# A scheduled attention-and-MLP kernel: the second products four tiles behind, new prices in the planner, variance's small steps on GpSimd

## The chip, the cores and the metric

The kernel runs on one core of a Trainium2 chip. The metric is device time in microseconds (us). The engines are TensorE (PE in the profile; PEld is its weight loading), VectorE (DVE), ScalarE (ACT), GpSimd (POOL) and the engine that issues most loads, SyncE (SP).

## What is computed

Two stages follow one another. The first is attention over 4 batches, 8 heads, 768 positions and 64 numbers a head: each query sees the keys less than 16 positions away, and 24 summary keys, one for each block of 32 positions (the maximum of the block's keys; its value is the mean of the block's values). The second takes the heads side by side as 3072 rows of 512 numbers.

```python
k_sum = k.reshape(B, H, nb, block, D).max(axis=3)
v_sum = v.reshape(B, H, nb, block, D).mean(axis=3)
scores_l = where(|i - j| < 16, scale * q @ k.T, -1e9)
scores_s = scale * q @ k_sum.T + log(block)
a = softmax(concat(scores_l, scores_s))
x = a @ concat(v, v_sum)               # 3072 x 512 after the heads are joined
h = x @ w_in                           # 512 -> 1024
solu = h * softmax(h)
ln = (solu - mean) / sqrt(var + 1e-6) * g_ln
out = ln @ w_out                       # 1024 -> 512
```

## The kernel before

**Tiles.** The 3072 rows are 24 tiles of 128 rows, six to a batch. Attention works in steps: a batch has three groups `g` of 256 queries, a group two steps `pp`, each for two pairs of heads. So there are 24 attention steps too. For a step, `scores` copies the windows of the keys from `kraw` and the block maxima from `ksum` into one buffer `kw` (lines 530 to 538), multiplies (`s`, line 551), adds the mask and takes the maximum (line 571), takes exponentials (line 579) and divides by the sum (line 586, recorded at lines 263 and 264). `values_turn` transposes the result on TensorE (`t`) and copies it (`at`); `values` multiplies by the values (`x`, line 646) and splits the product into a high and a low part (`xh`, `xl`, line 652).

**A tile of the second stage** has three parts. `first(t)` makes `h` as 24 matmuls into two PSUM banks, since each product is done three times, high by low, low by high and high by high (line 671). Then follow row maximum (681), exponential (686), the multiply by `h` and 1/sum (694), the subtraction of the mean in two halves (702 on GpSimd, or 704 on VectorE), the sum of squares (707), and the small steps on one number a row that give 1/std `y`: scale and add (709), power -0.5 on GpSimd (712), and one correction step on VectorE (714, 716, 718). `turn(t)` transposes the centred tile `he` (`lt`) and splits it into `lh` and `ll` (732). `second(t)` makes the 24 matmuls of the output (`o`, line 747), scales them by `y` (`os`, 752 or 754) and stores them. Only `os` needs `y`.

**Distance.** In the loop over `t`, `turn` is called for tile `t - LAG + 1` and `second` for `t - LAG`; `LAG` is 5. The centred tile stays in one of `NHE` = 6 buffers `he` until `turn` has read it. Up to `t` = 5 (`NEAR`) the order around `first` is another than after it. The `h` banks and the banks shared by `x` and `o` are given out by `place_h` and `place_x`.

**Weights** come as 64-bit numbers in 16 pieces. Each is put together, rounded and split by `rounded` (lines 343 to 362) and then by `split_w_in` or `split_w_out` (375, 377); the eight output pieces are prepared during tiles 0 to 3. For `w_in` the staging buffers are the `he` buffers.

**The order of the work is made by a planner, `Plan`.** Every operation is recorded with an engine, a cost in us, the buffers that it reads and writes, and sometimes other engines that could do it (`alt`). `issue` then goes through a simulated time: for each engine it takes the operation that can begin first, and among those the one that is due first by what TensorE needs. An operation with a choice goes where its begin plus its cost plus a surcharge (`DEAR`: VectorE 0.3, ScalarE 0.3, GpSimd nothing) is least. Operations marked `port` are taken not to run on VectorE and GpSimd at one time. The result is a fixed order for each engine. Where the planner sees TensorE free before 80 us, `keep_up` puts in matmuls on zeros (line 863).

**Loads** go through SP's queue in program order. A batch's keys are loaded as four pairs `p`, at the tiles that `load_at` gives, and their block maxima are taken (`key_blocks`, line 414) at the tiles in `blocks_at`. For batches 2 and 3, GpSimd adds up the rows of the values (`add_rows`, lines 476 and 480).

Of the kernel before, what the change touches and what calls it, by code (L numbers as in the profile page):

```python
# [37 lines left out]
LAG = 5  # L38
NHE = 6
EARLY = 3  # L40
MEANS = 2
NEAR = 6
# [29 lines left out]
class Plan:  # L72
# [6 lines left out]
    RATE = 400.0  # L79
# [4 lines left out]
    DEAR = {"dve": 0.3, "act": 0.3}  # L84
# [53 lines left out]
    def issue(self):  # L138
# [50 lines left out]
        while len(order) < len(self.ops):  # L189
            t, e, o = min(((x[0], e, x[1]) for e in ready for x in [take(e)] if x),  # L190
                          key=lambda x: (x[0], x[2].due))
            for f in o.can:
                ready[f] = [x for x in ready[f] if x[1] is not o]
            then.pop(e, None)
            if o.then:
                then[e] = o.then
            o.start, o.engine, (o.cost, o.fn) = t, e, o.can[e]
            o.end = free[e] = t + cost(e, o, t)
            if e == "dve" and o.port:
                held = o.end  # L200
            if o.nbytes:
                dma = max(dma, o.end + 1.0) + o.nbytes / self.RATE * 1e-3
                o.end = dma + 0.8
            order.append(o)
            for u in o.users:
                u.left -= 1
                if not u.left:
                    enter(u)
# [21 lines left out]
def attn_then_solu(ctx: ExitStack, tc: tile.TileContext, q, k, v, vr, vb, w_in, w_out, g_ln, out):  # L230
# [98 lines left out]
    def load_w(key, src, after=()):  # L329
        raw[key] = x = plan.buf(const, [P, 1024], I32, f"w{key}", 1, f"raw{key}")  # L330
        op(sp, 0.05, lambda: nc.sync.dma_start(out=x.ap, in_=src.bitcast(I32)), w=[x], nbytes=P * 4096,
# [68 lines left out]
    def load_keys(b, p, after=()):  # L400
# [4 lines left out]
        op(sp, 0.05, lambda: nc.sync.dma_start(out=x.ap[:, i], in_=k[b, pp, :, i]), w=[(x, i)], nbytes=P * SP * 4,  # L405
# [12 lines left out]
    def load_v_rows(b, i):  # L418
# [3 lines left out]
        op(sp, 0.05, lambda: nc.sync.dma_start(out=x.ap, in_=vr[b, i]), w=[x], nbytes=P * 4096)  # L422
# [17 lines left out]
    def mean_values_pe(b):  # L440
# [18 lines left out]
        for g in range(4):  # L459
            op(act, 0.06, lambda g=g: nc.scalar.dma_start(  # L460
# [3 lines left out]
    def add_rows(b, hh, i):  # L464
# [3 lines left out]
        op(sp, 0.05, lambda w=w: nc.sync.dma_start(out=x.ap[:n, :w], in_=vb[b, hh, :, i * w:(i + 1) * w]),  # L468
# [30 lines left out]
    def load_q(b, g, pairs=None, after=()):  # L499
# [4 lines left out]
        op(sp, 0.05, lambda: nc.sync.dma_start(out=x.ap[:, part], in_=q[b, g, :, part]),  # L504
# [3 lines left out]
    def load_v(b, g, after=()):  # L508
        vt[b, g] = x = plan.buf(sb, [P, G, DM], F32, "vt", 2, f"vt{b}_{g}")
        op(sp, 0.05, lambda: nc.sync.dma_start(out=x.ap, in_=v[b, g]), w=[x], nbytes=P * 8192,  # L510
           after=after)

    def load_v2(b, g):
        x, y = vt[b, g], vsum[b]

        return op(act, 0.06, lambda: nc.scalar.dma_start(
# [3 lines left out]
    def scores(b, g, pp, each=False):  # L520

        nm_ = f"{b}_{g}_{pp}"
        kw = plan.buf(sb, [P, 2, G, KC], F32, "kw", 2, "kw" + nm_)
        x, y, qs = kraw[b, pp], ksum[b, pp], qt[b, g]

# [6 lines left out]
        for i in range(2) if each else [None]:  # L532
            i0, i1 = (0, 2) if i is None else (i, i + 1)
            f = (i1 - i0) / 2
            copy([(e, c * f + (1 - f) * 0.15) for e, c in COPY_K], lambda i0=i0, i1=i1: kw.ap[:, i0:i1, :, :WIN],
                 lambda i0=i0, i1=i1: window(i0, i1), r=[x if i is None else (x, i)], w=[(kw, (i, 0))], port=True)
            copy([(e, c * f + (1 - f) * 0.15) for e, c in COPY_KS], lambda i0=i0, i1=i1: kw.ap[:, i0:i1, :, WIN:],
                 lambda i0=i0, i1=i1: maxima(i0, i1), r=[y if i is None else (y, i)], w=[(kw, (i, 1))], port=True)
# [7 lines left out]
        def mm(i):  # L546
            for up in range(G // 2):
                for cu in range(2):
                    for j in range(2):
                        u, n = 2 * up + cu, 2 * i + up  # L550
                        nc.tensor.matmul(  # L551
                            sc.ap[cu * QT:(cu + 1) * QT, j, n * KC:(n + 1) * KC],
                            qs.ap[j * D:(j + 1) * D, 2 * pp + i, u * QT:(u + 1) * QT],
                            kw.ap[j * D:(j + 1) * D, i, u, :], start=True, stop=True)
        if each:
            for i in range(2):
                op(pe, 0.66, lambda i=i: mm(i), r=[(qs, 2 * pp + i), (kw, (i, 0)), (kw, (i, 1))], w=[(sc, i)])
        else:
            yield 1.18, lambda: (mm(0), mm(1)), [(qs, 2 * pp), (qs, 2 * pp + 1), kw], [sc]
# [100 lines left out]
    def first(t):  # L660
# [15 lines left out]
        nm, nmu, ss, y2 = (sm(x) for x in ("hm", "nmu", "ss", "y2"))  # L676
# [23 lines left out]
        for hf in range(2):  # L700
# [4 lines left out]
                out=e.ap[:, sl], in0=e.ap[:, sl], scalar1=nmu.ap, scalar2=None, op0=ALU.add))])  # L705
# [3 lines left out]
        op(dve, 0.07, lambda: nc.vector.tensor_scalar(  # L709
            out=ss.ap, in0=ss.ap, scalar1=1.0 / DF, scalar2=1e-6, op0=ALU.mult, op1=ALU.add), w=[ss])  # L710

        op(pool, 0.46, lambda: nc.gpsimd.tensor_tensor(out=y.ap, in0=ss.ap, in1=mhalf, op=ALU.pow),
           r=[ss], w=[y])
        op(dve, 0.13, lambda: nc.vector.scalar_tensor_tensor(
            out=y2.ap, in0=y.ap, scalar=y.ap, in1=ss.ap, op0=ALU.mult, op1=ALU.mult), r=[y, ss], w=[y2])
        op(dve, 0.07, lambda: nc.vector.tensor_scalar(
            out=y2.ap, in0=y2.ap, scalar1=-0.5, scalar2=1.5, op0=ALU.mult, op1=ALU.add), w=[y2])
        op(dve, 0.07, lambda: nc.vector.tensor_tensor(out=y.ap, in0=y.ap, in1=y2.ap, op=ALU.mult),
           r=[y2], w=[y])
# [17 lines left out]
    def second(t):  # L737
# [3 lines left out]
        for cols in [slice(0, 256), slice(256, 512)] if t == NT - 1 else [slice(0, DM)]:  # L741
# [14 lines left out]
            op(act, 0.06, lambda os=os, cols=cols: nc.scalar.dma_start(  # L756
# [38 lines left out]
    load_at, blocks_at = ((0, 1, 2, 3), (-1, 0, 1, 1)), ((0, 1, 2, 3), (0, 1, 1, 2))  # L795

    def pairs(at, t):
        return [(b + 1, p) for b in range(B - 1) for p in range(NPAIR) if t == 2 * NG * b + at[b > 0][p]]

    step = lambda i: (*its[i // 2], i % 2)  # L800
    for t in range(NT):
# [3 lines left out]
        if not near:  # L805
            run(scores(*step(t + 2)))
# [100 lines left out]
```

## Time and profile before

| | us |
|---|---|
| runs of the kernel before | 416.07, 417.98, 419.96 (median 417.98) |
| the profiled execution | 415.89 |
| its span | 414.2 |
| first `h` matmul (line 671) begins | 34.74 |
| first `o` matmul (line 747) begins | 96.91 |

The page's span runs from the first to the last instruction. A row of a group has line, engine, operation, output <- input, shape and count; then the busy time in us and the mean duration in ns; then the idle time of the engine just before, and what ended it. A row of the timeline has begin and length in us. A row of a stretch has its begin and end, its length, the busy time of PE, PEld, DVE, ACT and POOL with the number of instructions, the granted TensorE clock, the share of the DMA engines and GB/s. A row of waits says who waited for whom: us in total, times, longest. [...]

### The profile page before, as it was taken

The numbers are of one execution on the slowest core, as the hardware profiler recorded it, in microseconds if no ns is written. First come the engines' busy times: TensorE is split into PE (matmuls) and PEld (weight loads), VectorE is DVE, ScalarE is ACT, GpSimd is POOL, SyncE is SP. The second block draws the span as 40 slices with busy tenths as digits, with TensorE's granted clock in tenths as the row PEclk, the third lists the DMA queues.
The fourth block names the chain that finished last, engine by engine and source line by source line (L and its number), as shares of the span: only waits on it lengthen the run. The fifth ranks groups of instructions, "written<-read, shape, count | busy, mean of one in ns | idle before, by whom it ended". The sixth has DMA issues, their size and how long they took to land.

```text
span 414.2 us, 9561 instructions
## 1 busy us (share of the span) xinstructions
PE 395.3 (95%) x3654; PEld 299.6 (72%) x3654; DVE 311.7 (75%) x1009; ACT 223.2 (54%) x699; POOL 95.6 (23%) x151
## 2 busy tenths in 40 slices
PE   7899998989996999998999999999999999999996
PEld 3347656557775788877878887788888888777776
DVE  3989988999999878678877768758867785667230
ACT  3967774958495574746547455564554622123110
POOL 4223204210579640125111011011101010111000
PEclk9999999999999899999999999999999999999999
DMA  7999991122393140264240410430400000000011
GB/s 270 413 413 349 339 360 45 53 103 71 112 349 113 41 180 2 75 205 116 83 145 18 138 53 27 154 65 26 121 29 27 25 2 27 25 27 25 27 51 52
DMA packets 14993, 49.23 MB, mean 119 GB/s; under 512 B 1836, under 2 KB 2092, under 8 KB 13412
## 3 DMA queue, kind: packets, MB, share of 16 engines
q1 hardware_dynamic: 10112, 40.12, 26.8%
q10 hardware_dynamic: 4836, 8.51, 6.9%
q8 instruction: 29, 0.48, 0.5%
q14 instruction: 16, 0.13, 0.1%
HBM read 40.11 MB, written 6.29 MB: 112 GB/s over the span
## 4 chain that ended last, share of the span: by engine, by line
PE 62%; DVE 4%; POOL 1%; DMA 1%; ACT 0%; issue 0%; DVEq 0%
PE o L747 29%; PE h L671 22%; PE x L646 3%; PE s L551 3%; PE lt L607 3%; PE t L607 2%; POOL st_v L476 1%; DMA st_v<-in_vb 1%; DVE ksum L414 1%; DVE he L694 0%; DVE ll L732 0%; DVE e L571 0%; DVE at L257 0%; DVE lh L257 0%; DVE hm L681 0%; DVE os L754 0%
## 5 line engine op out<-in xcount | busy, mean ns | idle before, releaser
L671 PE MATMUL h<-w,xh 128*128 128x512 f32 x384 | 128.8, 404 | 5.5 <-DVE he L694 5.3
L747 PE MATMUL o<-w,lh 128*128 128x512 f32 (+1 forms) x400 | 128.4, 392 | 0.3 <-DVE xl L652 0.3
L579 ACT ACTIVATE e<-e,nm 128x120 f32<-128x120 f32 x192 | 73.1, 385 | 36.3 <-DVE nm L571 36.1
L671 PEld LDWEIGHTS h<-w,xh 128*128 128x128 f32 x384 | 72.8, 189 | 26.9 <-DVE he L694 8.5
L747 PEld LDWEIGHTS o<-w,lh 128*128 128x128 f32 x400 | 74.0, 188 | 19.0 <-issue 2.1
L747 PE MATMUL o<-w,ll 128*128 128x512 f32 (+1 forms) x200 | 77.1, 386 | 0.0
L671 PE MATMUL h<-w,xl 128*128 128x512 f32 x192 | 76.1, 397 | 0.9 <-DVE xl L652 0.8
L702 POOL TENSOR_SCALAR he<-he,nmu 128x512 f32<-128x512 f32 x27 | 24.7, 918 | 112.7 <-DVE nmu L697 112.7
L681 DVE TENSOR_REDUCE hm<-h 128x1 f32<-128x512 f32 x48 | 32.8, 686 | 18.7 <-PE h L671 18.5
L671 PEld LDWEIGHTS h<-w,xl 128*128 128x128 f32 x192 | 36.5, 190 | 9.5 <-DVE xl L652 1.5
L747 PEld LDWEIGHTS o<-w,ll 128*128 128x128 f32 x200 | 37.6, 188 | 7.2
L686 ACT ACTIVATE he<-h,hm 128x512 f32<-128x512 f32 x48 | 32.7, 688 | 18.3 <-DVE hm L683 16.6
L256 ACT COPY at<-t 120x512 f32<-120x512 f32 x28 | 16.0, 586 | 48.9 <-PE t L607 34.5
L571 DVE CUSTOM_DVE_ANT_0 e<-s,mask 128x120 f32<-128x120 f32 x192 | 40.5, 275 | 0.0
L707 ACT ACTIVATE sq<-he 128x1024 bf16<-128x1024 f32 x24 | 25.2, 1051 | 24.3 <-POOL he L702 16.7
L579 ACT ACTIVATION_READ_ACCUMULATOR e<-e,nm 128x1 f32 x192 | 36.6, 191 | 0.0
L694 DVE SCALAR_TENSOR_TENSOR he<-h,hz,he 128x512 f32<-128x512 f32 x48 | 34.2, 744 | 0.2
L732 DVE TENSOR_TENSOR ll<-lt,lh 128x512 fp32r<-128x512 f32 x48 | 31.6, 678 | 1.2 <-ACT lh L256 1.2
L646 PE MATMUL x<-at,vt 120*64 120x64 f32 (+1 forms) x768 | 28.7, 226 | 1.8 <-ACT at L256 1.1
L257 DVE CAST lh<-lt 128x512 fp32r<-128x512 f32 x21 | 14.4, 688 | 20.9 <-ACT lh L256 20.8
L551 PE MATMUL s<-kw,qt 64*64 64x120 f32 x768 | 26.1, 272 | 3.9 <-POOL kw L258 1.8
L646 PEld LDWEIGHTS x<-at,vt 120*64 120x64 f32 (+1 forms) x768 | 24.7, 137 | 6.8 <-issue 2.2
(89 smaller groups left out, 507.9 us busy)
## 6 DMA issues: line engine op xcount, KB each, us to landing
vt<-in_v SPq DMA_DIRECT2D x12, 1024.0 KB, 6.9
kraw<-in_k SPq DMA_DIRECT2D x16, 400.0 KB, 9.3
out<-os ACTq DMA_DIRECT2D x23, 256.0 KB, 2.0
qt<-in_q SPq DMA_DIRECT2D x11, 512.0 KB, 5.1
raw<-in_w_in SPq DMA_DIRECT2D x8, 512.0 KB, 9.6
raw<-in_w_out SPq DMA_DIRECT2D x8, 512.0 KB, 9.4
st_v<-in_vr SPq DMA_DIRECT2D x6, 512.0 KB
st_v<-in_vb SPq DMA_DIRECT2D x8, 384.0 KB
```

Source lines behind the costliest of these rows:

```text
L551: nc.tensor.matmul(sc.ap[cu * QT:(cu + 1) * QT, j, n * KC:(n + 1) * KC], qs.ap[j * D:(j + 1) * D, 2 * pp + i, u * QT:(u + 1) * QT], kw.ap[ ...
L571: nc.vector.tensor_tensor_reduce(out=e.ap[:, n, :], in0=sc.ap[:, j, (2 * i + up) * KC:(2 * i + up + 1) * KC], in1=mask[:, mi, :], scale=-S ...
L579: nc.scalar.activation(out=e.ap[:, n, :], in_=e.ap[:, n, :], func=AF.Exp, bias=nm.ap[:, n:n + 1], scale=-1.0, accum_out=z.ap[:, n:n + 1])
L646: nc.tensor.matmul(xp()[j * D:(j + 1) * D, i, qs], vs.ap[:k, u, cs], at.ap[:k, u % 2, n[j] + u // 2, :], start=not apart, stop=not apart o ...
L671: nc.tensor.matmul(hp.ap, a.ap[:, c, ts], w.ap[:, i], start=(c == 0 and n == 0), stop=(c == NKC - 1 and n == 2))
L681: op(dve, 0.6, lambda i=i, hp=hp: nc.vector.tensor_reduce(out=nms.ap[:, i:i + 1], in_=hp.ap, op=ALU.max, axis=AX.X, negate=True), r=[hp], ...
L686: op(act, 0.71, lambda i=i, hp=hp: nc.scalar.activation(out=part(i), in_=hp.ap, func=AF.Exp, bias=nm.ap, accum_out=zs.ap[:, i:i + 1]), r=[ ...
L694: op(dve, 0.67, lambda i=i, hp=hp: nc.vector.scalar_tensor_tensor(out=part(i), in0=hp.ap, scalar=zs.ap[:, 0:1], in1=part(i), op0=ALU.mult, ...
L702: op(pool, 0.62, lambda sl=sl: nc.gpsimd.tensor_scalar(out=e.ap[:, sl], in0=e.ap[:, sl], scalar1=nmu.ap, scalar2=1.0, op0=ALU.add, op1=ALU ...
L707: op(act, 1.13, lambda: nc.scalar.activation(out=sq.ap, in_=e.ap, func=AF.Square, accum_out=ss.ap), r=[e], w=[sq, ss])
L732: op(dve, 0.6, lambda part=part, r=r: nc.vector.tensor_tensor(out=part(lo), in0=tp.ap[:, r], in1=part(hi).bitcast(F32), op=ALU.subtract), ...
L747: nc.tensor.matmul(o.ap[:, cols], a.ap[:, f, :], w.ap[:, i, cols], start=(f == 0 and n == 0), stop=(f == NFC - 1 and n == 2))
```

## The change

- `LAG` is 4 and `NHE` 5: `turn` and `second` are called one tile earlier, and there is one `he` buffer fewer.
- In the planner an issue of a load on SP costs 0.43 instead of 0.05, and issues on ScalarE's queue 0.34 or 0.8 instead of 0.06. Transfers run at 410 GB/s, or 270 in the first 6.9 us, instead of 400, and land 0.6 after their end instead of 0.8.
- The surcharges are VectorE 0.6, ScalarE 0.3, GpSimd 1.0.
- The subtraction of the mean may run on ScalarE too, and is marked `port`.
- Of the small steps of the variance, those that were on VectorE are on GpSimd: scale and add, three multiplies, one more scale and add, around the power that was there before. That makes five GpSimd instructions more and four VectorE instructions fewer for a tile.
- The first group's scores (batch 0, group 0) are made directly from `kraw` and `ksum`, with two matmuls in place of each one and without `kw`. `DIRECT` = 0 leaves all others as they were.
- `load_at` and `blocks_at` are worked out. For batch 1 the four loads stand at tiles 1, 2, 3, 3 instead of 0, 1, 2, 3 and the block maxima at 2, 3, 3, 4 instead of 0, 1, 2, 3; for batches 2 and 3 they come out as before.

The diff, without the further lines on which only 0.05 becomes 0.43:

```diff
@@ -35,10 +35,11 @@
...
-LAG = 5
-NHE = 6
+LAG = 4
+NHE = 5
...
+DIRECT = 0
@@ -76,12 +77,12 @@
...
-    RATE = 400.0
+    RATE, SLOW = 410.0, 270.0
...
-    DEAR = {"dve": 0.3, "act": 0.3}
+    DEAR = {"dve": 0.6, "act": 0.3, "pool": 1.0}
@@ -199,8 +200,9 @@
...
-                dma = max(dma, o.end + 1.0) + o.nbytes / self.RATE * 1e-3
-                o.end = dma + 0.8
+                dma = max(dma, o.end + 1.0)
+                dma += o.nbytes / (self.RATE if dma > self.COLD else self.SLOW) * 1e-3
+                o.end = dma + 0.6
@@ -328,7 +330,7 @@
...
-        op(sp, 0.05, lambda: nc.sync.dma_start(out=x.ap, in_=src.bitcast(I32)), w=[x], nbytes=P * 4096,
+        op(sp, 0.43, lambda: nc.sync.dma_start(out=x.ap, in_=src.bitcast(I32)), w=[x], nbytes=P * 4096,
@@ -457,7 +459,7 @@
...
-            op(act, 0.06, lambda g=g: nc.scalar.dma_start(
+            op(act, 0.34, lambda g=g: nc.scalar.dma_start(
@@ -501,27 +503,28 @@
...
-        op(sp, 0.05, lambda: nc.sync.dma_start(out=x.ap[:, part], in_=q[b, g, :, part]),
+        op(sp, 0.43, lambda: nc.sync.dma_start(out=x.ap[:, part], in_=q[b, g, :, part]),
...
-        op(sp, 0.05, lambda: nc.sync.dma_start(out=x.ap, in_=v[b, g]), w=[x], nbytes=P * 8192,
+        op(sp, 0.43, lambda: nc.sync.dma_start(out=x.ap, in_=v[b, g]), w=[x], nbytes=P * 8192,
...
-        return op(act, 0.06, lambda: nc.scalar.dma_start(
+        return op(act, 0.8, lambda: nc.scalar.dma_start(
...
-    def scores(b, g, pp, each=False):
+    def scores(b, g, pp, direct=False, each=False):
+
...
-        kw = plan.buf(sb, [P, 2, G, KC], F32, "kw", 2, "kw" + nm_)
...
+        kw = None if direct else plan.buf(sb, [P, 2, G, KC], F32, "kw", 2, "kw" + nm_)
@@ -529,13 +532,9 @@
...
-        for i in range(2) if each else [None]:
-            i0, i1 = (0, 2) if i is None else (i, i + 1)
-            f = (i1 - i0) / 2
-            copy([(e, c * f + (1 - f) * 0.15) for e, c in COPY_K], lambda i0=i0, i1=i1: kw.ap[:, i0:i1, :, :WIN],
-                 lambda i0=i0, i1=i1: window(i0, i1), r=[x if i is None else (x, i)], w=[(kw, (i, 0))], port=True)
-            copy([(e, c * f + (1 - f) * 0.15) for e, c in COPY_KS], lambda i0=i0, i1=i1: kw.ap[:, i0:i1, :, WIN:],
-                 lambda i0=i0, i1=i1: maxima(i0, i1), r=[y if i is None else (y, i)], w=[(kw, (i, 1))], port=True)
+        if kw:
+            copy(COPY_K, lambda: kw.ap[:, :, :, :WIN], lambda: window(0, 2), r=[x], w=[(kw, 0)], port=True)
+            copy(COPY_KS, lambda: kw.ap[:, :, :, WIN:], lambda: maxima(0, 2), r=[y], w=[(kw, 1)], port=True)
@@ -548,15 +547,19 @@
...
-                        nc.tensor.matmul(
-                            sc.ap[cu * QT:(cu + 1) * QT, j, n * KC:(n + 1) * KC],
-                            qs.ap[j * D:(j + 1) * D, 2 * pp + i, u * QT:(u + 1) * QT],
-                            kw.ap[j * D:(j + 1) * D, i, u, :], start=True, stop=True)
+                        ds = slice(j * D, (j + 1) * D)
+                        at = (g * G + u) * QT
+                        keys = [(0, x.ap[ds, i, at:at + WIN]), (WIN, y.ap[ds, i, :])] if direct else [(0, kw.ap[ds, i, u, :])]
+                        for c, ks in keys:
+                            c += n * KC
+                            nc.tensor.matmul(
+                                sc.ap[cu * QT:(cu + 1) * QT, j, c:c + ks.shape[-1]],
+                                qs.ap[ds, 2 * pp + i, u * QT:(u + 1) * QT], ks, start=True, stop=True)
...
-                op(pe, 0.66, lambda i=i: mm(i), r=[(qs, 2 * pp + i), (kw, (i, 0)), (kw, (i, 1))], w=[(sc, i)])
+                op(pe, 1.1, lambda i=i: mm(i), r=[(qs, 2 * pp + i), (x, i), (y, i)], w=[(sc, i)])
...
-            yield 1.18, lambda: (mm(0), mm(1)), [(qs, 2 * pp), (qs, 2 * pp + 1), kw], [sc]
+            yield 2.0 if direct else 1.18, lambda: (mm(0), mm(1)), [(qs, 2 * pp), (qs, 2 * pp + 1)] + ([x, y] if direct else [kw]), [sc]
@@ -673,7 +676,7 @@
...
-        nm, nmu, ss, y2 = (sm(x) for x in ("hm", "nmu", "ss", "y2"))
+        nm, nmu, ss = (sm(x) for x in ("hm", "nmu", "ss"))
@@ -702,21 +705,23 @@
...
-                out=e.ap[:, sl], in0=e.ap[:, sl], scalar1=nmu.ap, scalar2=None, op0=ALU.add))])
+                out=e.ap[:, sl], in0=e.ap[:, sl], scalar1=nmu.ap, scalar2=None, op0=ALU.add)),
+                (act, 0.57, lambda sl=sl: nc.scalar.activation(
+                    out=e.ap[:, sl], in_=e.ap[:, sl], func=AF.Identity, bias=nmu.ap))], port=True)
...
-        op(dve, 0.07, lambda: nc.vector.tensor_scalar(
+
+        mul = lambda to, x: op(pool, 0.3, lambda: nc.gpsimd.tensor_tensor(out=to.ap, in0=to.ap, in1=x.ap, op=ALU.mult), r=[x], w=[to])
+        op(pool, 0.3, lambda: nc.gpsimd.tensor_scalar(
...
-
...
-        op(dve, 0.13, lambda: nc.vector.scalar_tensor_tensor(
-            out=y2.ap, in0=y.ap, scalar=y.ap, in1=ss.ap, op0=ALU.mult, op1=ALU.mult), r=[y, ss], w=[y2])
-        op(dve, 0.07, lambda: nc.vector.tensor_scalar(
-            out=y2.ap, in0=y2.ap, scalar1=-0.5, scalar2=1.5, op0=ALU.mult, op1=ALU.add), w=[y2])
-        op(dve, 0.07, lambda: nc.vector.tensor_tensor(out=y.ap, in0=y.ap, in1=y2.ap, op=ALU.mult),
-           r=[y2], w=[y])
+        mul(ss, y)
+        mul(ss, y)
+        op(pool, 0.3, lambda: nc.gpsimd.tensor_scalar(
+            out=ss.ap, in0=ss.ap, scalar1=-0.5, scalar2=1.5, op0=ALU.mult, op1=ALU.add), w=[ss])
+        mul(y, ss)
@@ -753,7 +758,7 @@
...
-            op(act, 0.06, lambda os=os, cols=cols: nc.scalar.dma_start(
+            op(act, 0.34, lambda os=os, cols=cols: nc.scalar.dma_start(
@@ -770,11 +775,11 @@
...
-    op(sp, 0.05, lambda: nc.sync.dma_start(out=g_sb, in_=g_ln), w=[g_b], nbytes=P * 64)
+    op(sp, 0.43, lambda: nc.sync.dma_start(out=g_sb, in_=g_ln), w=[g_b], nbytes=P * 64)
...
-        run(scores(0, 0, pp, True))
+        run(scores(0, 0, pp, True, True))
@@ -792,10 +797,19 @@
...
-    load_at, blocks_at = ((0, 1, 2, 3), (-1, 0, 1, 1)), ((0, 1, 2, 3), (0, 1, 1, 2))
+    scored = lambda i: i - 2 if i - 2 < NEAR else max(NEAR - 1, i - 4)
+
+    load_at, blocks_at = {}, {}
+    for later in range(1, B):
+        for p in range(NPAIR):
+            t = scored(2 * NG * later + p // 2)
+            old = 2 * NG * (later - 1) + (2 * NG - 2 if p > 1 else -1)
+            free = scored(old) + (old - 2 >= NEAR) if old > 1 else 0
+            load_at[later, p] = max(t - (3, 2, 2, 2)[p], free)
+            blocks_at[later, p] = max(t - (2, 1, 2, 1)[p], load_at[later, p])
...
-        return [(b + 1, p) for b in range(B - 1) for p in range(NPAIR) if t == 2 * NG * b + at[b > 0][p]]
+        return [x for x in at if at[x] == t]
@@ -803,7 +817,7 @@
...
-            run(scores(*step(t + 2)))
+            run(scores(*step(t + 2), t < DIRECT))
```

More of the change, by code (lines that the diff above doesn't have):

```diff
@@ L404, in load_keys @@
         x = kraw[b, pp]
-        op(sp, 0.05, lambda: nc.sync.dma_start(out=x.ap[:, i], in_=k[b, pp, :, i]), w=[(x, i)], nbytes=P * SP * 4,
+        op(sp, 0.43, lambda: nc.sync.dma_start(out=x.ap[:, i], in_=k[b, pp, :, i]), w=[(x, i)], nbytes=P * SP * 4,
            after=after)
@@ L421, in load_v_rows @@
         vst[b, i] = x = plan.buf(sb, [P, 2, 512], F32, tag, 2, f"st_v{b}_{i}")
-        op(sp, 0.05, lambda: nc.sync.dma_start(out=x.ap, in_=vr[b, i]), w=[x], nbytes=P * 4096)
+        op(sp, 0.43, lambda: nc.sync.dma_start(out=x.ap, in_=vr[b, i]), w=[x], nbytes=P * 4096)
     def mean_values_first(b):
@@ L467, in add_rows @@
         n, w = NB * 4, BLOCK * D // 2
-        op(sp, 0.05, lambda w=w: nc.sync.dma_start(out=x.ap[:n, :w], in_=vb[b, hh, :, i * w:(i + 1) * w]),
+        op(sp, 0.43, lambda w=w: nc.sync.dma_start(out=x.ap[:n, :w], in_=vb[b, hh, :, i * w:(i + 1) * w]),
            w=[x], nbytes=P * 4096)
```

## The prediction

> **What bounds the kernel now.** I read the page's part 1 first, then busy time by stretches, because an average over stages with different limits says little.
>
> ```profile
> PE 395.3 (95%) x3654; PEld 299.6 (72%) x3654; DVE 311.7 (75%) x1009; ACT 223.2 (54%) x699; POOL 95.6 (23%) x151
> 60.00:134.00 74.00, 64.73 (x691) 46.65 (x690) 71.48 (x218) 51.53 (x166) 33.30 (x42) 1.00 0.39 126
> 205.00:335.00 130.00, 130.00 (x1250) 105.26 (x1248) 97.04 (x348) 69.15 (x237) 16.17 (x25) 1.00 0.21 70
> ```
>
> A stretch row gives its length, then PE, PEld, DVE, ACT and POOL busy. From 205 to 335 us TensorE has no gap: this half holds its own work, which the change neither removes nor adds to. Only reordering into earlier gaps can shorten it. The stretch 60 to 134 is another regime: VectorE is busy 71.48 of 74 us and TensorE is short by 74 - 64.73 = 9.27.
>
> ```profile
> PE h L671 <- DVE he L694: 5.3, 5, 2.7
> L863 PE MATMUL x<-zero 128*128 128x512 bf16 x22 | 5.1, 380 | 0.0
> L863 PE MATMUL t<-zero 128*128 128x512 bf16 x4 | 1.0, 382 | 0.0
> 133.80 7.26 PE h L671 x24
> 210.85 5.60 PE h L671 x24
> 34.74 0.50 PE L671 MATMUL h<-w,xh 128*128 128x512 f32 x1
> 11.68 7.73 PE L863 MATMUL vs_ps<-zero 128*128 128x512 bf16 x35
> ```
>
> These say what the gaps cost. In 60 to 134 TensorE's longest total wait is for VectorE's multiply at line 694, which frees a bank for the next `h`. 22 + 4 matmuls on zeros (line 863) fill another 5.1 + 1.0 us without doing work. After the longest gap the `h` group at 133.80 takes 7.26 where one in the steady part takes 5.60: 1.7 more. In all TensorE loses 9.3 + 6.1 + 1.7 = 17.1 us in that stretch. This is what the change can win at most there. Before the first `h` at 34.74 the start waits for loads and weight preparation; 7.7 us of zeros stand in it in one piece.
>
> **The change part by part.** All sums stand against the profiled execution (415.89 us: span 414.2 and 1.7 around it). The median shown is 2.1 above it, and I add that at the end.
>
> *Variance's small steps leave VectorE.* Rows of 35 to 134:
>
> ```profile
> L709 DVE TENSOR_SCALAR ss<-ss 128x1 f32<-128x1 f32 x6 | 0.7, 131 | 0.0
> L714 DVE SCALAR_TENSOR_TENSOR y<-y,ss 128x1 f32<-128x1 f32 x3 | 1.5, 498 | 0.0
> L716 DVE TENSOR_SCALAR y<-y 128x1 f32<-128x1 f32 x3 | 0.4, 124 | 0.0
> L718 DVE TENSOR_TENSOR y<-y,y 128x1 f32<-128x1 f32 x3 | 1.4, 457 | 0.0
> ```
>
> Together 4.0 us off the engine that is full. Neighbours overlap at their ends, so I take **-3.0** (bounds -1 and -4). Later VectorE is only 97.04 of 130 busy, and TensorE hides the saving.
>
> *The new prices move work from VectorE to ScalarE.* The planner's surcharge on VectorE rises from 0.3 to 0.6, ScalarE keeps 0.3, and line 702's subtraction may now run on ScalarE too.
>
> ```profile
> L704 DVE TENSOR_SCALAR he<-he,nmu 128x512 f32<-128x512 f32 x4 | 2.5, 619 | 0.0
> L345 DVE TENSOR_SCALAR cv<-raw 128x512 f32<-128x512 f32 x3 | 1.2, 415 | 0.0
> L351 DVE TENSOR_SCALAR cv<-raw 128x512 int32<-128x512 uint32 x2 | 1.8, 892 | 0.0
> L257 DVE COPY at<-t 120x512 f32<-120x512 f32 x5 | 3.4, 685 | 0.7 <-ACT at L256 0.7
> L257 DVE COPY kw<-kraw 128x768 f32<-128x768 f32 x3 | 2.4, 814 | 0.0
> L702 POOL TENSOR_SCALAR he<-he,nmu 128x512 f32<-128x512 f32 x8 | 7.3, 922 | 5.5 <-DVE nmu L697 5.5
> ```
>
> The five VectorE rows make 11.3 us that could go. ScalarE has 74 - 51.53 = 22.5 us free in 60 to 134, so there is room, even with line 702's eight halves from GpSimd on top. A move happens only where ScalarE can begin soon enough; I take half, **-5.6** (bounds 0 and -11.3).
>
> *Others move from GpSimd to VectorE.* GpSimd's surcharge goes from nothing to 1.0.
>
> ```profile
> L264 POOL TENSOR_TENSOR e<-e,z 128x960 f32<-128x960 f32 x4 | 7.4, 1860 | 16.4 <-DVE z L585 14.5 <-DVE y L716 2.0
> L263 DVE TENSOR_TENSOR e<-e,z 128x960 f32<-128x960 f32 x4 | 5.2, 1294 | 0.0
> L258 POOL COPY kw<-ksum 128x192 f32<-128x192 f32 x8 | 3.5, 438 | 26.1 <-PE s L551 16.9 <-DVE ksum L414 9.3
> 85.91 2.06 POOL L264 TENSOR_TENSOR e<-e,z 128x960 f32<-128x960 f32 x1 [3.19 <-DVE z L585]
> 86.24 2.28 DVE L377 SCALAR_TENSOR_TENSOR w<-cv,g_sb,w 128x512 fp32r<-128x512 f32 x1
> 109.15 0.73 DVE L377 SCALAR_TENSOR_TENSOR w<-cv,g_sb,w 128x512 fp32r<-128x512 f32 x1
> ```
>
> Four softmax multiplies cost VectorE up to 5.2 us; the eight `kw` copies have no row of their size on VectorE, so 0 to GpSimd's own 3.5. But a GpSimd multiply isn't free for VectorE today: beside the one at 85.91 a line 377 step takes 2.28, and 0.73 elsewhere, 1.55 lost. A multiply of 1.29 taken back is thus about even. Bounds -1 and +8.7; I take **+2.0**, mostly the copies, since the even multiply is the nearer row.
>
> *Five small steps more per tile on GpSimd.* Before, only the power runs there.
>
> ```profile
> 124.64 0.55 POOL L712 TENSOR_TENSOR y<-ss,mhalf 128x1 f32<-128x1 f32 x1 [0.16 <-DVE ss L709]
> L480 POOL TENSOR_TENSOR vacc<-vacc,st_v 96x64 f32<-96x64 f32 x1 | 0.3, 315 | 0.1
> ```
>
> No row shows a multiply of 128x1 on GpSimd. Bounds are nothing and the power's 0.55; the add of 96x64 is the nearest in kind, 0.31. Six variances (the row of line 709) make 30 steps before 134, 9.3 us of GpSimd's time (0 to 16.5). GpSimd is busy 33.30 of 74, so it has room on average. For VectorE the price is only what it is held up; between 0 and all 9.3 (16.5 at the power's price) I take **+2.0**, a fifth, as only some VectorE steps are stretched today: line 718 stands at 457 ns on average, its neighbour 716 at 124. The steady tiles hide it. The chain now waits for line 707's sum on GpSimd instead of VectorE; behind it in GpSimd's order stand `kw` copies, which TensorE's next `s` wants, and the row sums of the next batch. The results themselves are wanted four tiles later.
>
> *Products four tiles apart instead of five.*
>
> ```profile
> 96.91 0.50 PE L747 MATMUL o<-w,lh 128*128 128x512 f32 x1
> 205.06 5.79 PE o L747 x24
> 88.52 0.71 PE L607 MATMUL lt<-ident,he 64*128 64x64 f32 x16
> L732 DVE TENSOR_TENSOR ll<-lt,lh 128x512 fp32r<-128x512 f32 x5 | 3.3, 669 | 0.5 <-ACT lh L256 0.5
> L754 DVE TENSOR_SCALAR os<-o,y 128x512 f32<-128x512 f32 x2 | 1.5, 738 | 0.0
> ```
>
> The first `o` starts at 96.91. With a smaller distance one more `o` (5.8) with its transposes (0.6 net) comes within reach of the gaps: 6.4 us of TensorE time. VectorE pays two `ll` (1.3), half an `lh` (0.3, by the `at` copy of the same size) and an `os` (0.7) for it, 2.3 to 2.4. Net **-4.0**. Bounds: -6.4 if VectorE's part is hidden, 0 if the output weights come too late (the line 377 step at 109.15 is the last of them, already after the first `o` has begun). One `he` buffer fewer keeps one spare beside the four tiles in flight; I cost it at nothing, covered by the tile time: with five and a distance of four a buffer is still held for four. If that cover is gone, line 686 is late. The input weights are staged in the same buffers at the start, where VectorE takes the pieces one after another; that too I cost at nothing.
>
> *The start: scores straight from `kraw`, no `kw` copies.*
>
> ```profile
> L256 ACT COPY kw<-kraw 128x384 f32<-128x384 f32 (+1 forms) x7 | 4.4, 646 | 7.3 <-DMA kraw<-in_k 6.2 <-PE s L551 1.2
> 8.44 0.64 PE L551 MATMUL s<-kw,qt 64*64 64x120 f32 x16 [1.20 <-POOL kw L258]
> ```
>
> Four of these copies go (4 x 0.646 = 2.6 us of ScalarE). The four score groups double their matmuls, at most 4 x 0.64 = 2.6 more, in a place where zeros run otherwise. They begin a little sooner, but loads set the rest: **-0.5** (bounds -1.5 and +1.5).
>
> *Loads and their prices.* An SP issue now counts 0.43 in the plan; the transfers keep their program order except the next batch's keys.
>
> ```profile
> 2.62 0.43 SPq L504 DMA_DIRECT2D qt<-in_q  x1
> 59.45 0.94 DVE L414 TENSOR_REDUCE ksum<-kraw 128x24 f32<-128x768 f32 x1
> ```
>
> The new figure agrees with the trace's 0.43; it moves no work. Batch 1's key loads and their four reductions (3.7 us in all, from 59.45 on) stand one or two tiles later in the program. They still fall in the full stretch, and the four SP issues pass only q and v loads. I take 0 (bounds -1 and +1).
>
> Sum: -3.0 - 5.6 + 2.0 + 2.0 - 4.0 - 0.5 = **-9.1**, of 17.1 lost and a little in the start. 415.9 - 9.1 = 406.8; with 2.1 for the median, **409**.
>
> **The rivals.**
>
> *GpSimd holds VectorE; no change.* If every added step holds VectorE for its own length, as the multiply at 85.91 held line 377, the term +2.0 becomes 30 x 0.31 = +9.3 and the sum -1.8: 414.1, and **416.2** on the median. For it: 1.55 us lost beside one GpSimd instruction. Against it: GpSimd is busy 33.30 of the 74 us, so more than half of VectorE's steps there meet nobody. The Trainium skill, "SBUF — State Buffer", section "SBUF: two separate sides", states this as an exclusive lock: whichever of GpSimd and certain VectorE instructions (two-port modes or two SBUF inputs) starts first has the shared port pair for the whole instruction. By that rule it gives this rival's time if all collide; the row at 86.24 agrees with it.
>
> *The plan hardly differs.* If ScalarE is never free soon enough (0 instead of -5.6) and the output weights are late (0 instead of -4.0), what is left is -3.0 + 2.0 + 2.0 - 0.5 = +0.5: 416.4, **418.5** on the median. The 109.15 row speaks for it; ScalarE's 22.5 free microseconds against.
>
> *GpSimd becomes the bound, slower.*
>
> ```profile
> 110.00:135.00 25.00, 19.92 (x234) 15.66 (x231) 25.00 (x87) 17.92 (x58) 21.36 (x32) 0.97 0.68 222
> L712 POOL TENSOR_TENSOR y<-ss,mhalf 128x1 f32<-128x1 f32 x5 | 3.8, 757 | 0.6 <-DVE ss L709 0.6
> L702 POOL TENSOR_SCALAR he<-he,nmu 128x512 f32<-128x512 f32 x5 | 3.7, 744 | 0.3 <-DVE nmu L697 0.3
> ```
>
> In 110 to 135 GpSimd is busy 21.36 of 25 with the next batch's row sums, which are in order ahead of and behind the small steps. There five powers fall, so 25 new steps. Line 702 leaving takes 3.7 off and one multiply leaving 1.8: 15.9 + 25 x price. From 0.36 us a step it exceeds 25. At the power's 0.55 it is 29.6, 4.6 over: 1/std comes late, the scaled copy `os` waits, holds its bank, and `x` and `h` stand behind it. VectorE's saving is then hidden under GpSimd: 418.0 + 4.6 = **422.6**. For it: that full row. Against: 0.31 is nearer than 0.55, and 1/std is wanted tiles later.
>
> **How the numbers follow.** Forecast (399 to 413.8) 0.63; GpSimd holds VectorE, 0.13; the plan hardly differs, 0.11; GpSimd bound, 0.13. About 1% is what a measurement of this kernel tells from no change (its three runs span 416.07 to 419.96), so faster means under 413.8. The two middle rivals are "same", 0.24. If all 17.1 came back the time were 401; low 401.5. The upper end takes in both middle rivals, 418.8. Forecast's own range: 402 to 413.
>
> **What would show it.** Right: TensorE's gap in 60 to 134 falls from 9.3 to under 5 and the zeros there shrink; the first `o` starts before 96.9; line 702's halves are mostly on ScalarE, GpSimd keeps few of line 702; VectorE's total falls to about 285 to 295 and ScalarE's rises to 235 to 250; the new GpSimd steps read near 0.31. In the steady part an `o` keeps 5.8 and an `h` 5.6 us. Wrong: VectorE still full with stretched steps beside GpSimd's, TensorE waiting for `os` or a GpSimd line, or gaps appearing after 205 us, where a thinner distance of four would be to blame.

## The result: 406.02 us, 0.972 of the time before

| | before | changed kernel |
|---|---|---|
| runs, us | 416.07 to 419.96 | 405.13 to 406.69, median 406.02 |
| ratio to before, same chip | 1 | 0.9718, 95% interval 0.9667 to 0.9769 |
| profiled execution, us | 415.89 | 406.69 |
| its span, us | 414.2 | 404.9 |

The time lies 3.0 below the forecast of 409.0 and inside its range; the profiled execution came out at 406.69, where the sum had said 406.8. That agreement is luck, a meeting of errors: several terms are wrong, as the sections below show. Two single executions further below, 429.86 us of one kernel and 761.01 us of another, took far longer than the others of the same kernel and enter no ratio.

### The profile after

The page's part 1, and the two stretches of before again, with a third of 5 us:

```profile
PE 388.3 (96%) x3702; PEld 299.6 (74%) x3702; DVE 300.5 (74%) x933; ACT 230.5 (57%) x711; POOL 88.8 (22%) x231
```

```profile
60.00:134.00 74.00, 66.11 (x701) 50.41 (x700) 66.51 (x204) 56.34 (x164) 28.35 (x62) 0.95 0.40 128
205.00:335.00 130.00, 129.84 (x1280) 106.20 (x1280) 96.23 (x322) 70.69 (x240) 21.77 (x60) 1.00 0.21 70
95.00:100.00 5.00, 4.88 (x39) 3.54 (x40) 4.86 (x19) 2.04 (x3) 4.12 (x5) 0.50 0.45 139
```

VectorE is no longer full from 60 to 134: 66.51 of 74 where it had 71.48. TensorE's gap there fell only from 9.27 to 74 - 66.11 = 7.89. The granted clock is lower, 0.95 over the stretch and 0.50 from 95 to 100; in the kernel before it fell at the end of the stretch, to 0.63 from 134 to 138, where the `h` group of 7.26 stands. The stretch once more, with the matmuls on zeros alone (TensorE, its weight loads, clock):

```profile
60.00:134.00 74.00, 2.68 (x10) 0.81 (x10) 0.95 0.40 128
```

Zeros fell from 26 matmuls (6.1 us) to 10 (2.7). TensorE's loss there is now 7.9 gap + 2.7 zeros + about 2.4 of slow clock (half of the 4.88 busy at 0.50) = 13.0, against 17.1: 4.1 won. What it waits for, from 34.7 to 134, and then its timeline (begin, length):

```profile
PE o L752 <- DVE w L379: 4.8, 2, 2.6
PE s L555 <- issue: 1.3, 1, 1.3
```

```profile
74.81 0.50 PE L752 MATMUL o<-w,lh 128*128 128x512 f32 x1
91.98 0.49 PE L752 MATMUL o<-w,lh 128*128 128x512 f32 x1 [2.57 <-DVE w L379]
95.12 0.80 PE L752 MATMUL o<-w,lh 128*128 128x512 f32 x1 [2.18 <-DVE w L379]
96.70 1.88 PE L555 MATMUL s<-kw,qt 64*64 64x120 f32 x32
```

The first `o` begins at 74.81, 22 us sooner than before. Now the output weights are what is late: the wait for line 694's multiply (5.3) is gone, and one for line 379's split of `w_out` (4.8 in two pieces) stands in its place. After them an `o` matmul takes 0.80 instead of 0.50, and the score group of 32 takes 1.88, where the chain has 1.05 for the one at 73.83.

Where the end went is read from the chain:

```profile
210.29 5.60 PE h L674 x24
365.30 5.44 PE h L674 x24
390.53 11.31 PE o L752 x72
```

In the same view of before, the last `h` group begins at 367.31:

```profile
367.31 5.59 PE h L671 x24
```

The span is 9.3 shorter. Of these the last `h` begins 2.0 sooner, and 7.3 less stands behind it: one `o` product with its transposes (5.8 + 0.6 = 6.4) and 0.9 in small differences. By 210 us the lead is 210.85 - 210.29 = 0.6, with the one product more (6.4) already done: 7.0, of which the stretch 60 to 134 explains 4.1 and the first 60 us 0.9 (gap and zeros 24.0 before, 23.1 after). The other 2.0 I can't assign to a row. After 210 us another 1.4 is won. Of the eleven `h` groups before the last, five take 5.44 or 5.45 where all but one had taken 5.59 or 5.60, which makes 0.8; most of the rest stands in the `o` groups, which take 5.66 to 5.76 where they had taken 5.79 or 5.80.

### The profile page after: what moved, and what is told of

Read it like the earlier page. It is cut to its first block, busy times and chain, and to the rows that moved or that the text cites. A ratio compares the mean times of both kernels' runs of the same rounds, so it can differ in the third digit from the quotient of the medians.

```text
span 404.9 us, 9684 instructions
## 1 busy us (share of the span) xinstructions
PE 388.3 (96%) x3702; PEld 299.6 (74%) x3702; DVE 300.5 (74%) x933; ACT 230.5 (57%) x711; POOL 88.8 (22%) x231
## 4 chain that ended last, share of the span: by engine, by line
PE 71%; DMA 12%; DVE 11%; ACT 3%; issue 1%; POOL 1%; SPq 0%; ACTq 0%; POOLq 0%
PE o L752 32%; PE h L674 23%; PE x L649 5%; PE s L555 4%; DMA kraw<-in_k 3%; DMA qt<-in_q 3%; PE lt L610 3%; DMA raw<-in_w_in 2%; PE t L610 2%; DMA vt<-in_v 2%; DMA st_v<-in_vb 1%; DVE e L265 1%; DVE e L574 1%; DVE hm L684 1%; DVE ksum L416 1%
## 5 line engine op out<-in xcount | busy, mean ns | idle before, releaser
L674 PE MATMUL h<-w,xh 128*128 128x512 f32 x384 | 125.6, 396 | 0.0
L716 POOL TENSOR_SCALAR ss<-ss 128x1 f32<-128x1 f32 x24 | 6.4, 268 | 167.7 <-ACT sq L712 151.9
L674 PEld LDWEIGHTS h<-w,xl 128*128 128x128 f32 x192 | 36.1, 188 | 7.8 <-DVE xl L655 0.3
L265 DVE TENSOR_TENSOR e<-e,z 128x960 f32<-128x960 f32 x24 | 28.5, 1189 | 0.1
L478 POOL TENSOR_TENSOR st_v<-st_v 96x512 f32<-96x512 f32 (+3 forms) x28 | 22.1, 791 | 29.2 <-DMA st_v<-in_vb 28.5
```

The lines of the kernel that those rows point to most:

```text
L265: by = {dve: lambda: nc.vector.tensor_tensor(out=to(), in0=a(), in1=b(), op=kind), pool: lambda: nc.gpsimd.tensor_tensor(out=to(), in0=a() ...
L478: op(pool, 0.15 + w * 0.0021, lambda w=w, o=o: nc.gpsimd.tensor_tensor(out=o.ap[:n, :w], in0=x.ap[:n, :w], in1=x.ap[:n, w:2 * w], op=ALU.add),
L674: nc.tensor.matmul(hp.ap, a.ap[:, c, ts], w.ap[:, i], start=(c == 0 and n == 0), stop=(c == NKC - 1 and n == 2))
```

## The experiments

Each job ran four kernels and the kernel before on one chip. The first job had the distance alone, all but the distance, the variance back and the old surcharges; the second the old prices of loads, the old places of the keys, the first of the other plans and the kernel on ScalarE's wait; the third GpSimd free, the start with its copies, old keys and surcharges together, and the second other plan. The changed kernel was in none of these jobs, so it is compared by its ratio to before. Ratios have 95% intervals. Two kernels change nothing but the price at which the planner counts a wait; they show how far another order of the same work scatters.

### Another plan of the same work

```diff
-    SYNC = 0.13
+    SYNC = 0.14     # 0.12 in the second
```

> The changed kernel with one figure of the planner altered by a hundredth of a microsecond (its allowance between engines, 0.13 to 0.14), which means nothing on the chip. It measures what another plan of the same quality is worth. If effects of single parts are real at 3 us: within 1.5 of 406. If the plan is a matter of chance: 3 us or more away from 406.

> The changed kernel with the planner's allowance between engines at 0.12 instead of 0.13, again without meaning on the chip. With 0.14 the time was 405.5. If effects of 3 us of single parts are real: 404.5 to 407.5. If plans fall by chance: 3 us or more away from 406.

Measured: 405.5 us, 0.9676 (0.9615 to 0.9736), and 0.9676 (0.9626 to 0.9725), the second kernel's other executions between 403.08 and 405.72. So a plan shifted by a price of 0.01 lands up to 0.4% (1.8 us) from the changed kernel. A part whose undoing moves less than that isn't told from the scatter of plans. Two plans give only a least size of the scatter: that a larger difference is the part's own isn't shown by its size alone.

### The distance alone, and all but the distance

```diff
-LAG = 5          # first in the kernel before; then the reverse, in the changed one
-NHE = 6
+LAG = 4
+NHE = 5
```

> The kernel before, with the distance alone changed (LAG 4, NHE 5). My theory (VectorE's relief and the distance share the gain): 4 us faster than before, about 413.5, with the first o well ahead of 96.9. Rival 1 (the distance alone carries it, since the first o came 22 us earlier in the changed kernel): 406 to 408. Rival 2 (any new plan falls somewhere by chance): anywhere from 408 to 418, without relation to where the first o stands.

Measured: 409.65 us, 0.9814 (0.9788 to 0.9839), 7.8 less by the ratio than before's 417.56 in this job. The row of the `h` products in each kernel's view of that line (durations, first and last begin), before first, then this one:

```profile
L671 PE MATMUL h<-w,xh x384: 387/397/797, 34.7 to 372.5; 128*128 128x512 f32 x192
```

```profile
L671 PE MATMUL h<-w,xh x384: 388/394/628, 36.0 to 372.8; 128*128 128x512 f32 x192
```

The last `h` begins where it did (372.8, 372.5). The profiled span falls by 6.6 (414.2 to 407.6), which is the one product with its transposes (6.4) that no longer stands behind that point: it fitted into the gaps at no price.

> The changed kernel with the old distance (LAG 5, NHE 6), all else as changed. My theory: the 4 us of the distance are lost, about 410. Rival 1 (the distance alone carries it): 416 to 418. Rival 2 (chance of the plan): no relation, 404 to 414.

Measured: 408.81 us, 0.9787 (0.9762 to 0.9812). The same row in this kernel and in the changed one:

```profile
L674 PE MATMUL h<-w,xh x384: 387/394/628, 37.2 to 365.4; 128*128 128x512 f32 x192
```

```profile
L674 PE MATMUL h<-w,xh x384: 387/393/577, 36.3 to 370.4; 128*128 128x512 f32 x192
```

Without the distance the other parts bring the last `h` from 372.5 to 365.4, 7.1. With it the last `h` goes back to 370.4: the added product costs 5.0 of its 6.4 here. The stretch of the kernel without the distance, and its longest wait there:

```profile
60.00:134.00 74.00, 70.82 (x718) 51.30 (x717) 70.50 (x237) 59.72 (x194) 28.62 (x58) 0.98 0.39 124
PE s L555 <- DVE hz L692: 1.8, 1, 1.8
```

Its gap of 3.2 and its zeros of 6.3 leave 9.5 us there, so the gaps weren't used up. But it has no wait for line 379, where the changed kernel has 4.8. That fits the 5.0; that it is the cause isn't shown. Both together save 2.8%, the distance alone 1.9% and the rest alone 2.1%. They can't be added.

### The variance back on VectorE

```diff
-        mul = lambda to, x: op(pool, 0.3, lambda: nc.gpsimd.tensor_tensor(...
+        op(dve, 0.07, lambda: nc.vector.tensor_scalar(
...
+        op(dve, 0.13, lambda: nc.vector.scalar_tensor_tensor(
...
```

> The changed kernel with variance's small steps back on VectorE (four there, the power on GpSimd). My theory: 1 us slower, about 407 (3.0 back on VectorE, 2.0 of hold-ups less). If GpSimd's steps hold VectorE for their own length: 4 to 7 us faster, 399 to 402, with fewer stretched VectorE steps. Chance of the plan: up to 4 us either way.

Measured: 409.0 us, 0.9792 (0.9752 to 0.9831), 3.1 us more than the changed kernel by the ratios; the interval overlaps with that kernel's, not with those of the other two plans. The same holds for the kernel without the distance above. What TensorE waits for from 60 to 134:

```profile
PE lt L610 <- DVE he L707: 2.6, 1, 2.6
PE h L674 <- DVE he L697: 1.6, 1, 1.6
PE t L610 <- DVE e L265: 1.4, 1, 1.4
```

The waits are again for VectorE's large steps. The rival by which GpSimd's small steps hold VectorE falls: with them taken off GpSimd the time had to be 399 to 402. What they cost GpSimd in the changed kernel (groups, busy us and mean ns):

```profile
L716 POOL TENSOR_SCALAR ss<-ss 128x1 f32<-128x1 f32 x24 | 6.4, 268 | 167.7 <-ACT sq L712 151.9 <-DVE os L759 9.8 <-DVE ksum L416 5.8
L715 POOL TENSOR_TENSOR ss<-ss,y 128x1 f32<-128x1 f32 x48 | 13.9, 293 | 3.1
L722 POOL TENSOR_SCALAR ss<-ss 128x1 f32<-128x1 f32 x24 | 4.6, 192 | 1.7
L715 POOL TENSOR_TENSOR y<-y,ss 128x1 f32<-128x1 f32 x24 | 4.5, 191 | 1.7
```

The multiplies take 0.19 each at the median; the mean of 293 in the second row comes from a few long ones (longest 1136). In all, the 120 steps take 29.4 us, 0.245 each on average.

### The old surcharges, and GpSimd free of one

```diff
-    DEAR = {"dve": 0.6, "act": 0.3, "pool": 1.0}
+    DEAR = {"dve": 0.3, "act": 0.3}     # "dve": 0.6 in the second
```

> The changed kernel with the old surcharges (VectorE 0.3, ScalarE 0.3, GpSimd none). My theory: 3 to 4 us slower, about 409.6 (5.6 back on VectorE, 2.0 back on GpSimd), VectorE's busy time 60 to 134 back up by some 4 us. If the surcharges do nothing: 406. Chance of the plan: up to 4 us either way.

Measured: 403.23 us, 0.9648 (0.9616 to 0.968): 2.9 faster, where a loss was expected, and 1.2 faster than the two other plans, which is within the scatter. Its page:

```profile
PE 387.0 (96%) x3696; PEld 297.4 (74%) x3696; DVE 275.5 (68%) x879; ACT 230.4 (57%) x708; POOL 139.2 (34%) x288
```

ScalarE has 230.4 with the old surcharges and 230.5 with the new. So on balance they moved nothing from VectorE to ScalarE. They moved 25 us to VectorE (275.5 to 300.5), off GpSimd (139.2 to 88.8). The groups of the changed kernel, then those of before:

```profile
L265 DVE TENSOR_TENSOR e<-e,z 128x960 f32<-128x960 f32 x24 | 28.5, 1189 | 0.1
L707 DVE TENSOR_SCALAR he<-he,nmu 128x512 f32<-128x512 f32 x36 | 16.2, 483 | 0.7
L709 ACT ACTIVATE he<-he,nmu 128x512 f32<-128x512 f32 x11 | 7.8, 720 | 13.2 <-DVE nmu L700 13.2
L705 POOL TENSOR_SCALAR he<-he,nmu 128x512 f32<-128x512 f32 x1 | 1.7, 1701 | 6.0 <-DVE nmu L700 6.0
```

```profile
L702 POOL TENSOR_SCALAR he<-he,nmu 128x512 f32<-128x512 f32 x27 | 24.7, 918 | 112.7 <-DVE nmu L697 112.7
L263 DVE TENSOR_TENSOR e<-e,z 128x960 f32<-128x960 f32 x19 | 22.5, 1186 | 0.4
L704 DVE TENSOR_SCALAR he<-he,nmu 128x512 f32<-128x512 f32 x21 | 10.7, 512 | 0.6
```

Of 27 halves GpSimd keeps one; VectorE has 15 more than before and ScalarE 11, and all 24 softmax multiplies stand on VectorE. ScalarE's 7.3 us more than before (223.2 to 230.5) are about its 11 halves (7.8). With the old surcharges it has ten of them too, so the new choice of engine gave them to it, not the surcharge. TensorE's wait for line 379 from 60 to 134 falls from 4.8 to 0.4 with the old surcharges.

> The changed kernel with GpSimd's surcharge alone taken out (VectorE keeps 0.6). If it was GpSimd's surcharge that drew work back onto VectorE: VectorE's total falls from 300 to 275 or less, GpSimd's rises to 140 or more, and the time is 402 to 404 as with all old surcharges. If VectorE's 0.6 did the harm: VectorE stays near 300 and the time near 406.

Measured: 0.9937 (0.9893 to 0.998), its executions but one from 412.44 to 417.21. VectorE's total fell to 271.0, the lowest of all, and GpSimd's rose to 144.9, so GpSimd's surcharge is shown to be what fills VectorE. But the time is nearly that of before. Its first 34 us, below those of the changed kernel:

```profile
0.00:34.00 34.00, 30.03 (x310) 13.95 (x312) 27.02 (x77) 21.23 (x58) 7.11 (x29) 1.00 0.96 368
```

```profile
0.00:34.00 34.00, 29.77 (x224) 12.55 (x227) 19.10 (x62) 13.89 (x45) 8.11 (x32) 0.95 0.96 369
```

In the start it does less on VectorE and ScalarE (19.10 and 13.89 against 27.02 and 21.23); the first `h` begins at 38.1 (36.3), the first split of `w_out` at 66.6 (50.2), the last at 108.2 (94.3). A smaller VectorE total doesn't make the kernel faster where the order in the start suffers; why the planner ordered it so isn't settled.

### The old prices of loads

```diff
-    RATE, SLOW = 410.0, 270.0
+    RATE, SLOW = 400.0, 400.0
...
-                o.end = dma + 0.6
+                o.end = dma + 0.8
...
-        op(sp, 0.43, ...
+        op(sp, 0.05, ...
```

> The changed kernel with the old prices of load issues (0.05 on SP, 0.06 on ScalarE's queue), the old rate of 400 at all times and the old landing time of 0.8. My theory (the prediction put 0 here, bounds -1 and +1): 405 to 407. Rival (the plan knows better when data come, and that is a good part of the gain): 409 to 412, TensorE waiting longer at its loads in the first 60 us.

Measured: 409.88 us, 0.9793 (0.9736 to 0.9849): 3.1 slower than the changed kernel, 4.4 slower than the other plan in the same job. The edit leaves every operation as it is; only the order and the choice of engines come out another way. TensorE's waits from 60 to 134 begin with:

```profile
PE o L752 <- DVE w L379: 2.6, 2, 2.2
PE x L649 <- ACT at L258: 2.2, 2, 2.0
```

The time is the rival's, but the rival's sign hardly shows: in the first 60 us TensorE's wait for keys is 1.3 us instead of 0.7, and the first `h` begins at 36.1 (36.3). At 212.76 us this kernel is 2.5 behind the changed one's 210.29. Another 0.8 is lost up to the last `h` group, and there the `o` groups are slower. The rows are two of this kernel and then one `o` group of the changed kernel:

```profile
212.76 5.60 PE h L674 x24
221.54 5.79 PE o L752 x24
219.07 5.71 PE o L752 x24
```

### The old places of the keys

```diff
+    load_at.update({(1, p): (0, 1, 2, 3)[p] for p in range(NPAIR)})
+    blocks_at.update({(1, p): (0, 1, 2, 3)[p] for p in range(NPAIR)})
```

> The changed kernel with batch 1's key loads at tiles 0, 1, 2, 3 and block maxima there too, as before. My theory (0): 405 to 407. Rival (four reductions of 0.94 us at 60 us delay the first tiles): 2 to 4 us slower, 408 to 410.

Measured: 402.7 us, 0.9622 (0.9566 to 0.9677), 2.8 faster than the other plan of its job; its executions (402.47 to 404.79) all lie below that one's lowest (405.27). Those of the second other plan (403.08 to 405.72) they overlap, so this gain isn't told from the scatter of plans. The wait for line 379 falls, and the stretch is fuller:

```profile
PE o L752 <- DVE w L379: 2.9, 1, 2.9
```

```profile
60.00:134.00 74.00, 68.40 (x712) 52.17 (x713) 68.37 (x207) 58.23 (x173) 31.91 (x64) 0.98 0.43 134
```

This one wait stands behind a split that takes 2.33 us, beside a GpSimd multiply that begins with it, where the changed kernel's eight splits take at most 0.752:

```profile
90.83 2.33 DVE L379 SCALAR_TENSOR_TENSOR w<-cv,g_sb,w 128x512 fp32r<-128x512 f32 x1
90.83 1.79 POOL L266 TENSOR_TENSOR e<-e,z 128x960 f32<-128x960 f32 x1 [3.35 <-ACT w L377]
```

In the changed kernel the reduction of a key pair stands right ahead of the late split, as the timelines show, but it isn't what made the split late. The split subtracts what ScalarE's line 377 writes, and that ended only at 94.28:

```profile
93.56 0.72 ACT L377 ACTIVATE w<-cv,g_sb 128x512 fp32r<-128x512 f32 x1 [3.08 <-DVE cv L265]
93.38 0.95 DVE L416 TENSOR_REDUCE ksum<-kraw 128x24 f32<-128x768 f32 x1
94.31 0.75 DVE L379 SCALAR_TENSOR_TENSOR w<-cv,g_sb,w 128x512 fp32r<-128x512 f32 x1
```

### ScalarE's wait for a load

The changed kernel's ScalarE is idle for 3.1 us, with a DMA issue ahead in its order that waits for a load, before it can prepare the weights:

```profile
88.33 0.84 ACTq L518 DMA_DIRECT2D vt<-vsum  x1
89.21 0.66 ACT L345 ACTIVATE cv<-raw 128x512 f32<-128x512 f32 x1 [3.11 <-DMA vt<-in_v]
```

```diff
-        return op(act, 0.8, lambda: nc.scalar.dma_start(
+        return op(sp, 0.8, lambda: nc.sync.dma_start(
```

> The changed kernel with the copies of the summary values into vt issued on SP's queue instead of ScalarE's. In the changed kernel ScalarE's queue stands at such an issue until the load of vt has landed at 88.3 us; the weight step behind it is late, and TensorE waits 4.8 us for line 379 and then runs at half clock for some 3 us. My theory: that is what is lost there, and 4 to 7 us come back, 399 to 402. Rival (VectorE sets that time anyway): 405 to 407.

Measured: 405.79 us, 0.9691 (0.9635 to 0.9747). The theory falls: the time is that of the other plan beside it (405.5). ScalarE no longer waits there, and TensorE waits for VectorE all the same:

```profile
PE o L752 <- DVE w L379: 2.9, 2, 2.5
PE s L555 <- DVE ll L737: 1.6, 1, 1.6
```

### The start with its copies

`scores` and the calls at the start as they were before:

```diff
-        run(scores(0, 0, pp, True, True))
+        run(scores(0, 0, pp, True))
```

> The changed kernel with the start as before (kw copies for the first group's scores). The prediction's term: 0.5 slower, 405.5 to 407. Rival: the direct scores free ScalarE early and the weights come sooner, 2 to 4 us slower without them, first h after 37 us.

Measured: 402.8 us, 0.9631 (0.9583 to 0.968). Its stretch is fuller than the changed kernel's, 70.62, of which 3.0 are zeros:

```profile
60.00:134.00 74.00, 70.62 (x731) 53.09 (x732) 67.93 (x205) 62.00 (x186) 35.72 (x72) 0.98 0.41 136
```

But the other plan of its job, at 0.9676, has an interval and executions that overlap with these (401.07 to 404.52 against 403.08 to 405.72). So no gain of the direct scores shows, and that they cost something isn't shown either.

### Old keys and old surcharges together

Both edits shown above, `DEAR` and the places of batch 1's keys, in one kernel.

> The changed kernel with both parts undone that alone were faster than it (old places of batch 1's keys, 402.7, and old surcharges, 403.2). If the two gains stand beside each other: 399 to 401. If both fill the same gaps of TensorE in the first 134 us: 402 to 404. If they were plans by chance: 402 to 407.

Measured: 403.66 us, 0.9673 (0.9638 to 0.9709), no better than either edit alone. That fits the second reading, the same gaps, and the third, chance; these runs don't tell them apart. Four kernels (402.7, 402.8, 403.2, 403.7) lie below the changed one, and these runs separate them neither from each other nor from the second other plan.

## Why the prediction was right, and where it was wrong

| step | forecast | what the runs show |
|---|---|---|
| distance four | -4.0 | -7.8 alone; about -3 last, with all else in place |
| variance: off VectorE -3.0, on GpSimd +2.0 | -1.0 | about -3 |
| surcharges: to ScalarE -5.6, to VectorE +2.0 | -3.6 | +2.9 against the changed kernel, +1.2 against the other plans |
| loads' prices | 0 | about -3 |
| key places | 0 | +4.0 against the changed kernel, +2.8 by the medians against the plan beside it |
| start without copies | -0.5 | +3.6 against the changed kernel; within the scatter of plans |

The forecasts are on the profiled execution; the third column is, but for the first number, each edit undone in the changed kernel, by the ratios. The three values of about -3 are larger than the scatter of the two other plans, but the intervals behind them overlap with the changed kernel's, and the profiled spans give 1.3 for the distance last, 1.3 for the variance and 3.4 for the loads' prices. So their sizes are rough, and how much of each is a chance of the plan stays open. The column doesn't add up to the gain (9.3 in spans): the distance's product fitted into the gaps free of charge alone and cost 5.0 of 6.4 behind the other parts.

**The bound was read rightly.** The loss stood in 60 to 134, VectorE set it, and all of the 130 us after 205 stayed as full as before. The ceiling of 17.1 was not reached; 4.1 of it came back there.

**Distance: mechanism right, size too small.** The step that took off 2.4 for VectorE's part was wrong. The kernel with the distance alone has its last `h` unmoved, so the bound of 6.4, with VectorE's part hidden, was the price. The warning beside it, that the output weights may come too late, came true in the changed kernel, with 4.8 us of waits for line 379. The kernel with the distance alone and the one without the distance have no such wait.

**Surcharges: the step that failed.** "A move happens only where ScalarE can begin soon enough; I take half" took VectorE's own rows as what would move. ScalarE's surcharge was below VectorE's, but GpSimd's rose by more, and its work went to VectorE first. VectorE's 311.7 less the 19.5 of the variance's rows over the whole run would be 292.2; it reads 300.5. The signs named for this (VectorE 285 to 295, ScalarE 235 to 250, line 702 mostly on ScalarE) failed; only that GpSimd keeps few of line 702 held.

**Small steps: price and hold-ups put too high.** GpSimd's price of 0.31 was taken from an add of 96x64; the 128x1 steps take 0.245 on average, and 0.19 at the median of the multiplies. The fifth that I charged VectorE for (+2.0) doesn't show: putting the steps back costs 3.1, as much as the whole saving that was forecast for VectorE. The rival that GpSimd becomes the bound, from 0.36 a step, falls by the same 0.245; GpSimd is busy 14.05 of the 25 us from 110 to 135. A single VectorE step is still stretched, but beside the row sums of the values and not beside a small step:

```profile
95.75 2.03 DVE L265 TENSOR_TENSOR e<-e,z 128x960 f32<-128x960 f32 x1
95.50 2.88 POOL L478 TENSOR_TENSOR st_v<-st_v 96x512 f32<-96x512 f32 x2 [13.98 <-DMA st_v<-in_vb]
```

It takes 1.19 on average, so 0.84 is lost. That is what the lock in the Trainium skill, "SBUF — State Buffer", section "SBUF: two separate sides", would give; as a price of the small steps, it isn't seen.

**Loads at nothing: wrong. Key places at nothing: not settled.** "It moves no work" is true of the loads and false of the plan, which puts other work in order around them: with the old prices the kernel is 4.4 slower than the other plan beside it. Of batch 1's four reductions two begin at 53.70 and 56.24, ahead of the stretch and earlier than the first in the kernel before (59.45), and only the other two fall in it, at 68.48 and 93.38. That they delay the `w_out` splits isn't shown, and the gain of their old places is within the scatter of plans.

**Signs that held:** the first `o` before 96.9, zeros shrunk, no gaps after 205 us. **Signs that failed:** the gap under 5 (7.9), the small steps near 0.31, the `h` of 5.6 in the steady part (five of eleven at 5.44 or 5.45), and the totals above.

## What to carry to other kernels

A change to a planner's prices is a change of order: look for what is cheapest after the new surcharge, not for what the surcharge names, and time a neighbouring plan or two to know the scatter (here at least 0.4%) before crediting a part. Parts that fill the same gaps aren't terms of a sum: bound their total by the gap, and size each one both alone and last. When a product can be pulled into earlier gaps, count what then stands behind the last step of the other kind; that row (372.5 against 372.8) told the whole gain of the distance.

## What the chip showed that I had not expected

- Small GpSimd steps are cheap: 0.19 us at the median for a 128x1 multiply, against 0.55 for the power.
- Two idle stretches of 2.57 and 2.18 us, with three records of `o` matmuls between them, were followed by a granted clock of 0.50 for some 5 us. The kernel before has such a pair too: 1.08 and 2.71 us with one score group between them, and 0.63 from 134 to 138. In the kernel with the old key places, after one such wait of 2.9, the clock was 0.79 from 90 to 95 and 0.87 from 95 to 100.
- In the steady part some groups of 24 matmuls are quicker than others, on the same data at a granted clock of 1.00. The `o` groups take 5.79 or 5.80 in the three kernels with the old prices of loads (before, the distance alone, the old prices), and 5.64 to 5.77 in all others. The `h` groups stay at 5.59 or more in the kernel before and in three later ones without a surcharge on GpSimd (old surcharges, GpSimd free, old keys and surcharges); with the distance alone some take 5.50, in the changed kernel 5.44. The cause is open.
- Executions of one kernel differ with their mean granted clock: with GpSimd free of a surcharge 412.44 us at 1.000 and 417.21 at 0.988. The changed kernel's four stand at 0.987 to 0.995.
